# An attention and channel-mix kernel whose first six tiles are laid out by hand

## The chip, the cores and the metric

The kernel runs on one core of a Trainium2 chip. A core has five engines that work side by side: TensorE (PE; its weight loads are listed apart as PEld), VectorE (DVE), ScalarE (ACT), GpSimd (POOL) and SyncE (SP, which here only issues transfers). The metric is the device time of one execution, in microseconds (us), as the median of several runs.

## The reference

Attention over 4 sequences of 768 tokens with 8 heads of 64, then a channel mix of the kind that RWKV models use. Cut to what matters:

```python
# attention: q, k, v are (4, 8, 768, 64); n_global = 8, n_local = 96
scores = (1 / sqrt(64)) * q @ k.transpose()
keep = is_global | is_local                # the first 8 keys, and the 96 keys up to the query
scores = where(keep, scores - slopes[h] * dist, -1e9)
a = exp(scores - max(scores))
a = a / (sum(a) + 1e-9)
x = a @ v                                  # heads side by side: (4, 768, 512)

# channel mix: w_k (512, 1024), w_r (512, 512), w_v (1024, 512), all float64
x_prev = x shifted by one token (0 before the first)
xk = mu_k * x + (1 - mu_k) * x_prev
xr = mu_r * x + (1 - mu_r) * x_prev
out = sigmoid(xr @ w_r) * (relu(xk @ w_k)**2 @ w_v)
```

## The kernel before

**Attention** goes by 24 tiles of 128 queries, each in four pairs of heads (hp). Tile n has 128 new keys; its window is 256 keys wide (128 where a sequence begins): the 32 first of the sequence, 96 before the tile, and its own. In the first 7 tiles ("native") queries and keys are float32 on 64 of 128 partitions (`qz`, `kz`; the other 64 rows are zero), and each tile loads its own 128 keys and those before anew into its half of a two-buffer `kz`. For a pair, `scores` makes the product (L287), DVE adds the bias and finds the maximum (L295, `e<-s,pat`), ACT takes exp and its sum (L296). After every second pair DVE forms r = 1 / (sum + 1e-9) (L302, L303) and POOL multiplies the four e by it (L306). `transposes` turns e on PE (`t`, L317) and ACT copies it out of PSUM (`et`, L318); `weighted` multiplies with v (`av`, L334), and ACT copies a tile's `av` to `x` (L345).

**The weights** come as float64 and are taken apart by bit operations in 20 steps of 128x512: 8 of w_k, 4 of w_r, 8 of w_v. `weight_begin` loads the raw words, ACT takes |top| times a power of two (L166, L169), then POOL (L167, first 8) or DVE (L170, the other 12) scales or bounds it, and DVE makes three bit operations: a shift (L171), the sign (L172) and the low word's bits (L173). ACT or POOL rounds the result to float32r, the hi part; `weight_end` has POOL subtract for the lo part (L180). `weights_go` sets how many are begun and ended after each slot.

**The channel mix** goes by 12 chunks of 256 tokens. `mix` makes xk and xr from x (POOL L357, or ACT for chunk 0; DVE L358), with hi (L359) and lo parts (L360). Each product is three matmuls, hi with hi, hi with lo and lo with hi (L371 to L373): 96 for xk @ w_k (`kp`), then relu and square (L397, L398), 24 for xr @ w_r (`z`), 48 for the product with w_v (`vps`), and the output (L414). This is a generator that yields 40 times in a chunk.

**What sets the order.** The main loop has 25 steps of four slots; slot = 4 * step + hp. In each slot come, in the program, the transposes of the tile before, the scores of this tile and then up to 5 yields of channel mix, by a budget (`run_ffn(2.5)` twice). Chunk c's mix is queued at hp 0 of step 2c + 3; for the first, the budget begins at -17.5. From this program a scheduler with a timeline of its own sets the order of each engine's instructions: one may go ahead of those written before it. Waits between engines follow from the buffers: among others 3 PSUM tiles of the pool `f` (kp, z, vps), 2 for the transposes and 1 for av; and the 3 buffers of `p4k` in SBUF, which the mixes, the queries and keys from tile 7 on and the raw w_r and w_v weights share.

Of the kernel before, what the change touches and what calls it, by code (L numbers as in the profile page):

```python
# [33 lines left out]
def tile_biased_attention_channel_mix(ctx: ExitStack, tc: tile.TileContext, qT, kT, v, n_sizes, mu_kr, w_k, w_v, w_r, q_rows, k_rows, v_rows, slopes, out):  # L34
    nc = tc.nc
    vec, act, pool, pe = nc.vector, nc.scalar, nc.gpsimd, nc.tensor
# [106 lines left out]

    def weight_begin(i):
        # A float64 weight's words: (sign, 11 exponent bits, 20 bits), (32 bits).
        # a: its first 24 significant bits as a float32; hi: a rounded to float32r; lo: the rest of a.
# [1 line left out]
        if name != "k":
            raw = p4k.tile([128, 512, 2], I32, tag="t4k", name=f"w64_{i}")
            a = f2_pool.tile([128, 512], I32, tag="f2", name=f"wa_{i}")  # L150
        elif k < 2:
            both = f_pool.tile([128, 2048], I32, tag=("kk_hi", "kk_lo")[k], name=f"w64_{i}")
            raw = both[:, 0:1024].rearrange("p (n w) -> p n w", w=2)
            a = both[:, 1024:1536]
        else:
            t = "xk" if k == 2 else "xr"
            raw = f_pool.tile([128, 512, 2], I32, tag=t + "_hi", name=f"w64_{i}")
            a = f_pool.tile([128, 512], I32, tag=t + "_lo", name=f"wa_{i}")
        nc.sync.dma_start(raw.rearrange("p n w -> p (n w)"), src[k * 128 : (k + 1) * 128, 2 * c : 2 * c + 1024])
# [4 lines left out]
        # or the min) to a large number, under 2**-127 (by underflow or the max) to 0.
        if i < 8:
            act.activation(a.bitcast(F32), top.bitcast(F32), AF.Abs, scale=2.0**111)  # L166
            pool.tensor_scalar(a.bitcast(F32), a.bitcast(F32), 2.0**-112, 2.0**-111, op0=ALU.mult, op1=ALU.mult)  # L167
        else:
            act.activation(a.bitcast(F32), top.bitcast(F32), AF.Abs, scale=2.0**16)  # L169
            vec.tensor_scalar(a.bitcast(F32), a.bitcast(F32), 2.0, HUGE, op0=ALU.max, op1=ALU.min)  # L170
        vec.tensor_scalar(a, a, 3, 0x7FFFFFF8, op0=ALU.logical_shift_left, op1=ALU.bitwise_and)  # L171
        vec.scalar_tensor_tensor(a, top, -0x80000000, a, op0=ALU.bitwise_and, op1=ALU.bitwise_or)  # L172
        vec.scalar_tensor_tensor(a, low, 29, a, op0=ALU.logical_shift_right, op1=ALU.bitwise_or)  # L173
# [8 lines left out]
    w_count = [0, 0]  # L182

    def weights_go(begun, ended):
        while w_count[0] < min(begun, len(w_steps)):
            weight_begin(w_count[0])
            w_count[0] += 1
        while w_count[1] < min(ended, w_count[0]):
            weight_end(w_count[1])
            w_count[1] += 1  # L190
# [8 lines left out]
    state = {}  # L199
    # the first tiles' queries and keys, with 64 rows of zeros: products of all 128 rows keep the tensor engine's clock up  # L200
    padded = []
    for i in range(2):
        qz = q_pool.tile([128, H, 128], F32, name=f"qz_{i}", tag="qh")
        kz = kw_pool.tile([128, H, 256], F32, name=f"kz_{i}", tag="kw")
        pool.memset(qz[64:128], 0.0)
        pool.memset(kz[64:128], 0.0)
        padded.append((qz, kz))
# [431 lines left out]
```

## Time and profile before

| what | value |
|---|---|
| median of 3 runs | 526.14 us (525.98 to 527.11) |
| span of the profiled execution | 524.1 us, 9900 instructions |
| PE busy | 495.9 us (95%) |
| DVE busy | 372.4 us (71%) |
| ACT busy | 323.6 us (62%) |
| POOL busy | 283.0 us (54%) |
| data moved | 48.16 MB, 92 GB/s over the span |

The profiled execution is one run of its own, and all places in time below are from its start. An engine's busy share is a mean over the whole span; where in the span an engine is full, and where another waits for it, is read from slices and windows. PE's instructions overlap, so the time of one in a row is read from its start to the start of the next. A row names the line of the program, the engine, the operation, then output and inputs by the program's names with their shapes.

### The profile page before, as it was taken

Reading aid. Unit: us, or ns where it says so; the run is one execution under the profiler, and the core shown is the slowest. Engines: PE = TensorE matmul, PEld = TensorE weight load, DVE = VectorE, ACT = ScalarE, POOL = GpSimd, SP = SyncE. Lnnn points to the kernel's source line nnn. Section 1 sums busy time; section 2 is a strip of 40 time slices with the busy share of each in tenths; the row PEclk is TensorE's granted clock in tenths of the full one; section 3 lists DMA queues with packets and bytes.
Section 4 is the critical chain, followed back from the end, with each engine's and each line's share of the span. In section 5 each row is a group of like instructions: output and inputs, shape, how many; then the busy total and the mean of one; then the engine's idle time right before and its main releaser. Section 6 shows DMA issues by size and latency. Waiting matters only on the chain.

```text
span 524.1 us, 9900 instructions
## 1 busy us (share of the span) xinstructions
PE 495.9 (95%) x3466; PEld 427.2 (82%) x3466; DVE 372.4 (71%) x854; ACT 323.6 (62%) x730; POOL 283.0 (54%) x410
## 2 busy tenths in 40 slices
PE   7885888979999999999999999999999999999995
PEld 4563766869898898898898898898898898898984
DVE  6799999987677766767767867767777865535321
ACT  4868585823957856846847757756757667643220
POOL 8799977987355644544547645535547634203000
PEclk9979799999999999999999999999999999999999
DMA  8998268150350530530521431521422210000101
GB/s 197 322 232 198 67 185 188 41 144 20 107 134 6 141 107 5 157 91 8 162 76 38 130 86 34 133 86 59 124 62 66 62 46 26 35 12 2 41 1 44
DMA packets 27304, 48.16 MB, mean 92 GB/s; under 512 B 7216, under 2 KB 13360, under 8 KB 27248
## 3 DMA queue, kind: packets, MB, share of 16 engines
q1 hardware_dynamic: 27104, 47.46, 34.0%
q8 instruction: 29, 0.48, 0.4%
q14 instruction: 27, 0.22, 0.1%
q10 hardware_dynamic: 144, 0.00, 0.0%
HBM read 41.16 MB, written 6.29 MB: 91 GB/s over the span
## 4 chain that ended last, share of the span: by engine, by line
PE 80%; DVE 11%; POOL 5%; issue 3%; DMA 1%; ACT 0%; DVEq 0%; POOLq 0%
PE vps L372 8%; PE vps L373 8%; PE vps L371 8%; PE kp L371 8%; PE kp L373 8%; PE kp L372 8%; PE av L334 7%; PE t L317 6%; PE z L371 4%; PE z L373 4%; PE z L372 4%; PE s L290 3%; PE s L289 3%; POOL e L306 2%; PE s L287 2%
## 5 line engine op out<-in xcount | busy, mean ns | idle before, releaser
L306 POOL TENSOR_SCALAR e<-e,r 128x256 f32<-128x256 f32 (+1 forms) x192 | 106.1, 570 | 137.0 <-DVE r L303 91.9
L371 PE MATMUL kp<-xk_hi,wk_hi 128*128 128x256 f32 x384 | 108.0, 282 | 0.2 <-DVE kk L398 0.2
L373 PE MATMUL kp<-xk_hi,wk_lo 128*128 128x256 f32 x384 | 107.5, 280 | 0.5 <-POOL wk_lo L180 0.5
L372 PE MATMUL kp<-xk_lo,wk_hi 128*128 128x256 f32 x384 | 107.3, 279 | 0.0
L296 ACT ACTIVATE e<-e,nmax 128x256 f32<-128x256 f32 (+1 forms) x192 | 92.6, 484 | 22.0 <-DVE nmax L295 21.0
L295 DVE CUSTOM_DVE_ANT_0 e<-s,pat 128x256 f32<-128x256 f32 (+1 forms) x192 | 69.0, 395 | 31.0 <-PE s L290 21.2
L372 PE MATMUL vps<-wv_lo,kk_hi 128*128 128x512 f32 x192 | 76.0, 396 | 2.6 <-POOL wv_lo L180 2.6
L371 PE MATMUL vps<-wv_hi,kk_hi 128*128 128x512 f32 x192 | 75.9, 395 | 0.4 <-POOL wv_hi L196 0.4
L373 PE MATMUL vps<-wv_hi,kk_lo 128*128 128x512 f32 x192 | 75.8, 395 | 0.0
L371 PEld LDWEIGHTS kp<-xk_hi,wk_hi 128*128 128x128 f32 x384 | 72.9, 190 | 1.2 <-DVE kk L398 0.6
L373 PEld LDWEIGHTS kp<-xk_hi,wk_lo 128*128 128x128 f32 x384 | 72.8, 190 | 0.9 <-POOL wk_lo L180 0.9
L372 PEld LDWEIGHTS kp<-xk_lo,wk_hi 128*128 128x128 f32 x384 | 72.9, 190 | 0.6
L318 ACT COPY et<-t 128x512 f32<-128x512 f32 (+1 forms) x96 | 52.0, 546 | 20.2 <-PE t L317 19.7
L317 PE MATMUL t<-ident,e 128*128 128x128 f32 x352 | 57.5, 280 | 5.7 <-POOL e L306 5.6
L398 DVE TENSOR_TENSOR kk<-kp,kk 128x512 f32<-128x512 f32 x48 | 33.1, 689 | 41.2 <-ACT kk L397 41.0
L317 PEld LDWEIGHTS t<-ident,e 128*128 128x128 f32 x352 | 41.2, 141 | 19.1 <-POOL e L306 9.2
L334 PE MATMUL av<-et,va 128*64 128x128 f32 x704 | 49.4, 284 | 0.6 <-ACT et L318 0.6
L334 PEld LDWEIGHTS av<-et,va 128*64 128x64 f32 x704 | 40.3, 139 | 10.5 <-issue 5.8
L400 DVE TENSOR_TENSOR kk_lo<-kk,kk_hi 128x512 fp32r<-128x512 f32 x48 | 35.3, 735 | 17.4 <-ACT kk_hi L399 17.3
L399 ACT CAST kk_hi<-kk 128x512 fp32r<-128x512 f32 x48 | 29.8, 622 | 25.6 <-DVE kk L398 25.6
L397 ACT ACTIVATE kk<-kp 128x512 f32<-128x512 f32 x48 | 28.3, 590 | 26.7 <-PE kp L373 24.5
L372 PEld LDWEIGHTS vps<-wv_lo,kk_hi 128*128 128x128 f32 x192 | 36.0, 187 | 10.5 <-POOL wv_lo L180 3.1
(103 smaller groups left out, 1051.1 us busy)
## 6 DMA issues: line engine op xcount, KB each, us to landing
kraw<-in_kT_dram SPq DMA_DIRECT2D x36, 256.0 KB, 3.9
qraw<-in_qT_dram SPq DMA_DIRECT2D x34, 256.0 KB, 4.1
va<-in_v_dram SPq DMA_DIRECT2D x24, 256.0 KB, 3.1
out_dram<-sig SPq DMA_DIRECT2D x24, 256.0 KB, 3.5
w<-in_w_k_dram SPq DMA_DIRECT2D x8, 512.0 KB, 9.1
w<-in_w_v_dram SPq DMA_DIRECT2D x8, 512.0 KB, 3.5
kz<-in_kT_dram SPq DMA_DIRECT2D x8, 256.0 KB, 6.7
w<-in_w_r_dram SPq DMA_DIRECT2D x4, 512.0 KB, 9.3
```

What stands on the lines that cost most here:

```text
L295: vec.tensor_tensor_reduce(out=e[:, :w], in0=o, in1=p[:, h, :], op0=ALU.add, op1=ALU.min, scale=-0.125, scalar=3.0e38, accum_out=s["nmax"] ...
L296: act.activation(e[:, :w], e[:, :w], AF.Exp, bias=s["nmax"][:, h : h + 1], scale=-1.0, accum_out=s["sum"][:, h : h + 1])
L306: pool.tensor_scalar(e[:, :w], e[:, :w], r[:, u : u + 1], 1.0, op0=ALU.mult, op1=ALU.mult)
L317: pe.transpose(pt[:, c : c + 128], e[:, k * 128 : (k + 1) * 128], ident)
L318: act.copy(et[:, : 2 * nb * 128], pt[:, : 2 * nb * 128])
L334: pe.matmul(o, vt[:, h * 64 : (h + 1) * 64], et[:, c : c + 128], start=k == 0, stop=k == nb - 1)
L371: pe.matmul(o, sh, mh, start=first, stop=False)
L372: pe.matmul(o, sh, ml, start=False, stop=False)
L373: pe.matmul(o, sl, mh, start=False, stop=last)
L398: vec.tensor_mul(kk, pv, kk)
L399: act.copy(kkh[:, 2 * fp : 2 * fp + 2, :], kk)
L400: vec.tensor_sub(kkl[:, 2 * fp : 2 * fp + 2, :], kk, kkh[:, 2 * fp : 2 * fp + 2, :])
```

## The change

It has seven parts.

1. DVE, ACT, POOL and SP are reached through a class `InOrder`; while its flag is on (slots 0 to 23, tiles 0 to 5) each of their instructions stays in the order in which the program is written. PE is still ordered by the scheduler. Since all calls pass through the class, their rows bear its one line, L46.
2. The weights go in four stages (load, begin, bits, end), each paced by a table, `w_pace`: a weight a slot up to slot 8, more behind it. Raw words are loaded three weights ahead.
3. The bits of a weight go through a PSUM tile, `wb`, of the pool `f`: the shift writes it, the sign operation reads and writes it, the last reads it and writes SBUF. All 20 weights are begun on ACT and POOL; L170 is gone.
4. In tiles 0 to 7 e is not multiplied by r. Instead r (128 queries x 8 heads) is spread by eight small products with the identity (`rb`), ACT copies that to SBUF (`rs`), and DVE multiplies `av` by it on the way to x, in place of ACT's copy.
5. The keys of tiles 0 to 6 lie in a ring of three tiles and are loaded once. POOL copies the 32 first keys aside (`k_glob`) and over the first 32 of the tile before. A head's scores are two products of 128 columns.
6. Chunk 0's mix is made in two halves of 128 tokens, through PSUM (`mix_first`), at slots 8 and 11. Up to step 8 a tile's av is made in its own next step, pair by pair; chunk c's channel mix is queued at slot 4 * (2c + 2) + 3 (c up to 3) or, later, at hp 0 of step 2c + 3; the budget starts at 0 for chunk 0 and at -10 for chunk 1.
7. A tile's queries and keys are loaded two steps ahead.

```diff
+EARLY = 8
+class InOrder:
+    on = True
+    def __getattr__(self, name):
+        f = getattr(self.engine, name)
+        def call(*args, **kwargs):
+            ins = f(*args, **kwargs)
+            if InOrder.on:
+                self.tc.keep_in_program_order(ins)
+            return ins
+        return call
...
+    def weight_load(i):
+        name, src, k, c = w_steps[i]
+        if i >= 7:
+            raw = p4k.tile([128, 512, 2], I32, tag="t4k", name=f"w64_{i}")
...
+    def weight_bits(i):
...
-        if i < 8:
-            act.activation(a.bitcast(F32), top.bitcast(F32), AF.Abs, scale=2.0**111)
-            pool.tensor_scalar(a.bitcast(F32), a.bitcast(F32), 2.0**-112, 2.0**-111, op0=ALU.mult, op1=ALU.mult)
-        else:
-            act.activation(a.bitcast(F32), top.bitcast(F32), AF.Abs, scale=2.0**16)
-            vec.tensor_scalar(a.bitcast(F32), a.bitcast(F32), 2.0, HUGE, op0=ALU.max, op1=ALU.min)
-        vec.tensor_scalar(a, a, 3, 0x7FFFFFF8, op0=ALU.logical_shift_left, op1=ALU.bitwise_and)
-        vec.scalar_tensor_tensor(a, top, -0x80000000, a, op0=ALU.bitwise_and, op1=ALU.bitwise_or)
-        vec.scalar_tensor_tensor(a, low, 29, a, op0=ALU.logical_shift_right, op1=ALU.bitwise_or)
+        bits = ps_f.tile([128, 512], I32, name=f"wb_{i}", tag="f")
+        vec.tensor_scalar(bits, a, 3, 0x7FFFFFF8, op0=ALU.logical_shift_left, op1=ALU.bitwise_and)
+        vec.scalar_tensor_tensor(bits, top, -0x80000000, bits, op0=ALU.bitwise_and, op1=ALU.bitwise_or)
+        vec.scalar_tensor_tensor(a, low, 29, bits, op0=ALU.logical_shift_right, op1=ALU.bitwise_or)
...
+    k_ring = [kz[0][:, 0], kz[0][:, 1], kz[1][:, 0]]
+    k_glob = kz[1][:, 1, :, 0:GMAX]
...
+            if t == 0:
+                pool_copy(k_glob[0:64], s["kr"][0:64, :, 0:GMAX])
+            elif t > 1:
+                pool_copy(state[n - 1]["kr"][0:64, :, 0:GMAX], k_glob[0:64])
...
-                pe.matmul(o, s["qr"][:, h, :], s["kr"][:, h, c0:256], start=True, stop=True)
+                for i, m in enumerate((n - 1, n) if t else (n,)):
+                    pe.matmul(o[:, i * 128 : (i + 1) * 128], s["qr"][:, h, :], state[m]["kr"][:, h, :], start=True, stop=True)
...
+        if n < EARLY:
+            if hp == 3:
+                r = s["r"] = s_pool.tile([128, H], F32, name=f"r_{n}", tag="rr")
+                vec.tensor_scalar(r, s["sum"], 1.0e-9, None, op0=ALU.add)
+                vec.reciprocal(r, r)
+            return
...
+        if hp == 2 and n < EARLY:
+            rb = ps_t.tile([128, 4, 128], F32, name=f"rb_{n}", tag="t")
+            for h in range(H):
+                a, o = divmod(h, 2)
+                pe.matmul(rb[64 * o : 64 * o + 64, a, :], s["r"][:, h : h + 1].to_broadcast([128, 64]), ident, start=True, stop=True)
+            s["rs"] = et_pool.tile([128, 4, 128], F32, name=f"rs_{n}", tag="et")
+            act.copy(s["rs"], rb)
...
+            if n < EARLY:
+                vec.tensor_mul(xo, av, s["rs"])
+            else:
+                act.copy(xo, av)
...
+    def mix_first(i):
...
+        for tag in "kr":
+            tmp[tag] = ps_f.tile([128, 4, 128], F32, name=f"mixp_{tag}", tag="f")
+            for j in range(4):
+                act.activation(tmp[tag][:, j, :], x[:, j, 128 * i : 128 * i + 128], AF.Copy, scale=mu[tag][1][:, j : j + 1])
+        for tag in "kr":
+            for j in range(4):
+                vec.scalar_tensor_tensor(tmp[tag][:, j, :], x[:, j, 128 * i + 1 : 128 * i + 129], mu[tag][0][:, j : j + 1], tmp[tag][:, j, :], op0=ALU.mult, op1=ALU.add)
+        for tag in "kr":
+            act.copy(first_mix[tag][0][:, :, c], tmp[tag])
+        for tag in "kr":
+            vec.tensor_sub(first_mix[tag][1][:, :, c], tmp[tag], first_mix[tag][0][:, :, c])
...
+    def go_ffn(c):
+        queue.append(ffn(c))
+        if c == 1:
+            budget[0] = -10.0
+    def w_pace(slot):
+        return slot + 1 if slot < 8 else 8 + (slot - 7) * 4 // 3 if slot < 11 else 12 + (slot - 10) * 8 // 5
...
+            slot = 4 * step + hp
+            InOrder.on = slot < 24
+            if step <= EARLY:
+                weights_go(3, w_pace(slot - 2))
+                weights_go(1, w_pace(slot))
+                if step:
+                    transposes(step - 1, hp)
+                weights_go(2, w_pace(slot - 1))
+                scores(step, hp)
+                if slot == 8:
+                    mix_first(0)
+                if step:
+                    for i in ([] if hp == 0 else [hp - 1]) + ([3] if hp == 3 else []):
+                        weighted(step - 1, i)
+                    if hp == 3:
+                        global_v(step)
+                        if step % 2 == 0:
+                            go_ffn(step // 2 - 1)
...
+            if hp == 3 and step + 2 < NTILES:
+                load_tile(step + 2)
+            if hp == 3 and 2 < step + 1 < NTILES:
+                load_v(step + 1)
+            weights_go(0, w_pace(slot) + 3)
```

How the order moves, at three places.

On PE, at the first `kp` (numbers behind the names are the program's own). Before:

```order
L334 MATMUL av_729<-et_3_676,va_413 64x128
L317 MATMUL t_0_750<-ident,e_0_582 128x128 x2
L371 MATMUL kp<-xk_hi,wk_hi 128x256 x2
L317 MATMUL t_0_750<-ident,e_1_585 128x128 x2
L317 MATMUL t_1_812<-ident,e_2_634 128x128 x2
L317 MATMUL t_1_812<-ident,e_3_637 128x128 x2
L372 MATMUL kp<-xk_lo,wk_hi 128x256
L373 MATMUL kp<-xk_hi,wk_lo 128x256
```

And after the change:

```order
L381 MATMUL av_505<-et_3_557,va_201 64x128
L356 MATMUL t_0_683<-ident,e_0_444 128x128 x2
L356 MATMUL t_0_683<-ident,e_1_447 128x128 x2
L356 MATMUL t_1_751<-ident,e_2_499 128x128 x2
L356 MATMUL t_1_751<-ident,e_3_502 128x128 x2
L441 MATMUL kp<-xk_hi,wk_hi 128x256
L442 MATMUL kp<-xk_lo,wk_hi 128x256
L443 MATMUL kp<-xk_hi,wk_lo 128x256
```

Before, the av of tiles 0 to 2 and the scores of tiles 0 to 3 and of three quarters of tile 4 stand ahead of the first kp, and 48 kp follow before the next attention. Now tiles 0 and 1 whole, tile 2's scores and half of its transposes stand ahead of it, and 72 kp follow.

On DVE, between the last e ahead of the first kp's inputs and the first result of kp. Before (w_5, wa_355 and wa_505 are weights):

```order
L172 SCALAR_TENSOR_TENSOR wa_355<-w_7_354,wa_355 128x512
L302 TENSOR_SCALAR r_3_691<-sum_476 128x4
L170 TENSOR_SCALAR wa_505<-wa_505 128x512
L173 SCALAR_TENSOR_TENSOR wa_355<-w_7_354,wa_355 128x512
L303 RECIPROCAL r_3_691<-r_3_691 128x4
L360 TENSOR_TENSOR xk_lo<-mix_k,xk_hi 128x1024
L171 TENSOR_SCALAR wa_505<-wa_505 128x512
```

And after (wb is a weight's bits in PSUM, w_12 the raw words of the thirteenth weight):

```order
L46 RECIPROCAL r_584<-r_584 128x8
L46 TENSOR_TENSOR x_415<-av_505,rs_596 128x4x128
L46 SCALAR_TENSOR_TENSOR mixp_k<-x_415,mus,mixp_k 128x128 x4
L46 SCALAR_TENSOR_TENSOR mixp_r<-x_415,mus,mixp_r 128x128 x4
L46 TENSOR_TENSOR xk_lo<-mixp_k,xk_hi 128x4x128
L46 TENSOR_TENSOR xr_lo<-mixp_r,xr_hi 128x4x128
L46 TENSOR_TENSOR kk<-kp,kk 128x512
L46 TENSOR_TENSOR kk_lo<-kk,kk_hi 128x512
L46 TENSOR_SCALAR wb_690<-wa_553 128x512
```

Before, the bits of the weights 5, 7 and 11 lie around xk_lo and go on behind it; now the bits of all twelve w_k and w_r weights stand ahead of it, and w_v's behind the first kk.

On PE, at the last chunk's kp near the end, behind the av of the last tile. Before:

```order
L371 MATMUL vps<-wv_hi,kk_hi 128x512
L372 MATMUL vps<-wv_lo,kk_hi 128x512
L373 MATMUL vps<-wv_hi,kk_lo 128x512
L371 MATMUL kp<-xk_hi,wk_hi 128x256
L372 MATMUL kp<-xk_lo,wk_hi 128x256
```

And after:

```order
L441 MATMUL vps<-wv_hi,kk_hi 128x512
L442 MATMUL vps<-wv_lo,kk_hi 128x512
L443 MATMUL vps<-wv_hi,kk_lo 128x512
L441 MATMUL kp<-xk_hi,wk_hi 128x256 x3
L442 MATMUL kp<-xk_lo,wk_hi 128x256
```

Between the last av and this kp, 6 z and 48 vps stood before; now 15 vps do.

More of the change, by code (lines that the diff above doesn't have):

```diff
@@ L142, in tile_biased_attention_channel_mix @@
     w_live = {}
-    def weight_begin(i):
-        name, src, k, c = w_steps[i]
[L148 to L154, printed above, removed]
-        else:
[L156 to L159, printed above, removed]
+    w_raw = {}
@@ new lines, in weight_load @@
+    def weight_load(i):
+        name, src, k, c = w_steps[i]
+        if i >= 7:
+            raw = p4k.tile([128, 512, 2], I32, tag="t4k", name=f"w64_{i}")
+        elif i < 3:
+            raw = p4k.tile([128, 512, 2], I32, tag="t4k", name=f"w64_{i}")
+        else:
+            both = f_pool.tile([128, 1024 if i < 5 else 2048], I32, tag=("xk_hi", "xr_hi", "kk_lo", "kk_hi")[i - 3], name=f"w64_{i}")
+            raw = both[:, 0:1024].rearrange("p (n w) -> p n w", w=2)
+        sync.dma_start(raw.rearrange("p n w -> p (n w)"), src[k * 128 : (k + 1) * 128, 2 * c : 2 * c + 1024])
+        w_raw[i] = raw
@@ L180, in weight_end, with weights_go @@
         pool.tensor_sub(lo, w_live.pop(i).bitcast(F32), hi)
[L182 to L190, printed above, removed]
+    w_stages = (weight_load, weight_begin, weight_bits, weight_end)
+    w_count = [0, 0, 0, 0]
+    def weights_go(stage, n):
+        while w_count[stage] < min(n, len(w_steps)):
+            w_count[stage] += 1
+            w_stages[stage](w_count[stage] - 1)
     def weights_need(n):
-        weights_go(n, n)
+        for stage in range(4):
+            weights_go(stage, n)
     def pool_copy(dst, src):
@@ L199, in tile_biased_attention_channel_mix @@
     state = {}
-    padded = []
+    qz = [q_pool.tile([128, H, 128], F32, name=f"qz_{i}", tag="qh") for i in range(2)]
+    kz = [kw_pool.tile([128, 2, H, 128], F32, name=f"kz_{i}", tag="kw") for i in range(2)]
     for i in range(2):
[L203 to L207, printed above, removed]
+        pool.memset(qz[i][64:128], 0.0)
+        pool.memset(kz[i][64:128], 0.0)
@@ L463, in tile_biased_attention_channel_mix @@
                 split_tile(step + 1)
[L464 to L466 removed]
+            if hp == 3 and step + 2 < NTILES:
[3 more added lines that the diff above has]
+            weights_go(0, w_pace(slot) + 3)
     for i in range(4):
         weighted(NTILES - 1, i)
[L469 to L470 removed]
+    go_ffn(NCHUNK - 1)
     while queue:
```

127 lines of the change are left out of this document (69 added, 58 removed).

## The prediction

> **What bounds the kernel now.** I read the page's span and its forty slices first, then a table of windows cut where TensorE's state changes, then the groups of the first 117 us. The page:
>
> ```profile
> span 524.1 us, 9900 instructions
> ...
> PE   7885888979999999999999999999999999999995
> ```
>
> A slice is 13.1 us, a digit its busy tenths. PE is at 9 from the tenth slice to the last but one, and below it before. In windows (columns: start:end and length, then busy us and count of PE, PEld, DVE, ACT, POOL, granted clock, DMA share, GB/s):
>
> ```profile
> 0.00:54.80 54.80, 41.10 (x209) 27.69 (x209) 47.00 (x149) 38.42 (x111) 47.94 (x67) 0.91 0.96 227
> 54.80:65.00 10.20, 8.62 (x57) 7.95 (x56) 8.92 (x18) 5.19 (x15) 10.20 (x12) 0.83 0.26 86
> 65.00:78.00 13.00, 11.32 (x88) 8.76 (x87) 13.00 (x35) 10.48 (x26) 9.07 (x11) 1.00 0.62 169
> 78.00:91.00 13.00, 10.49 (x90) 8.85 (x89) 13.00 (x28) 7.07 (x21) 9.97 (x12) 1.00 0.83 200
> 104.00:117.00 13.00, 9.91 (x61) 7.87 (x61) 11.50 (x15) 1.80 (x3) 10.36 (x11) 1.00 0.46 122
> 117.00:518.50 401.50, 401.49 (x2912) 355.62 (x2908) 265.26 (x588) 249.12 (x534) 183.37 (x287) 1.00 0.25 69
> ```
>
> The first cut is the first channel-mix product (kp) at 54.8. In the start VectorE (DVE) and GpSimd (POOL) are busier than PE: it is theirs, the rest is PE's. Behind it PE idles 1.58 + 1.68 + 2.51 + 3.09 = 8.9 us in four of the windows up to 117 (it is full in the one left out, 91 to 104), and none from 117 to 518.5. So the span is T0, the start of the first kp, plus the PE work behind it, plus PE's waits behind it. Before: 54.8 + 469.3. What fills the start (busy us and mean ns of one, then the idle time before):
>
> ```profile
> L306 POOL TENSOR_SCALAR e<-e,r 128x256 f32<-128x256 f32 x40 | 32.0, 814 | 8.4 <-DVE r L303 8.4
> L173 DVE SCALAR_TENSOR_TENSOR wa<-w,wa 128x512 int32<-128x512 int32 x16 | 15.1, 948 | 0.0
> L172 DVE SCALAR_TENSOR_TENSOR wa<-w,wa 128x512 int32<-128x512 int32 x16 | 12.6, 795 | 0.1
> L171 DVE TENSOR_SCALAR wa<-wa 128x512 int32<-128x512 int32 x16 | 8.5, 535 | 0.0
> ```
>
> POOL's normalisation of e and DVE's bit operations are the two large blocks, and both are edited.
>
> **The change in terms of this sum.** It shortens the start (no L306 in eight tiles, no L170, bits through PSUM, one load per key), fixes DVE's, ACT's and POOL's order to the 24th slot, and starts chunk 0's channel mix a slot earlier in the program, behind two whole tiles of attention where before four tiles' scores stood. What leaves the path ahead of T0 in this way has to be done behind it, where PE is the bound.
>
> *Work behind T0.* PE's rows:
>
> ```profile
> 25.03 1.03 PE L287 MATMUL s<-kz,qz 128*128 128x256 f32 x4
> 25.99 0.66 PE L334 MATMUL av<-et,va 128*64 128x128 f32 x8
> 54.79 0.48 PE L371 MATMUL kp<-xk_hi,wk_hi 128*128 128x256 f32 x2
> 59.38 0.41 PE L373 MATMUL kp<-xk_hi,wk_lo 128*128 128x256 f32 x1
> 59.59 0.41 PE L371 MATMUL kp<-xk_hi,wk_hi 128*128 128x256 f32 x1
> 63.07 0.28 PE L373 MATMUL kp<-xk_hi,wk_lo 128*128 128x256 f32 x1
> 63.19 0.28 PE L371 MATMUL kp<-xk_hi,wk_hi 128*128 128x256 f32 x1
> 93.17 0.60 PE L287 MATMUL s<-kz,qz 128*128 128x128 f32 x4
> 93.61 0.60 PE L317 MATMUL t<-ident,e 128*128 128x128 f32 x4
> 94.14 0.65 PE L334 MATMUL av<-et,va 128*64 128x128 f32 x4
> 166.99 1.95 PE av L334 x32
> ```
>
> From start to start, a score instruction of 256 columns takes 0.24 us (0.96 / 4) and one of 128 columns 0.11; a tile has 16 or 32 of them, 3.84 or 3.52 us. A transpose takes 0.13 (0.53 / 4), an av instruction 0.061 (1.95 / 32). Behind T0 now come 1.75 more tiles of scores (tile 3 and three quarters of tile 4, 6.7 us), ten transposes (1.25) and tile 2's av (1.95): +9.9. The product of r with the identity has the shape of an av instruction: 16 in a tile, six tiles behind T0, 16 x 6 x 0.061 = +5.9. Splitting the scores saves 0.32 in each of tiles 3 to 5: -1.0. Off go the waits of before, 8.9, and its slow kp: 33 at 0.21 (59.38 to 59.59) where one takes 0.12 (63.07 to 63.19), 3.1 us. So 469.3 - 12.0 + 9.9 + 5.9 - 1.0 = 472.1, and the span after is **T0 + 472.1 + S**, S being PE's new waits and slow stretches. It is even with before at T0 + S = 52.0.
>
> *T0.* In DVE's new order the first kp stands behind the bits of all twelve w_k and w_r weights, though the first kp reads only w_k's. DVE's rows:
>
> ```profile
> 9.78 0.28 DVE L295 CUSTOM_DVE_ANT_0 e<-s,pat 128x128 f32<-128x128 f32 x1
> 9.99 0.28 DVE L295 CUSTOM_DVE_ANT_0 e<-s,pat 128x128 f32<-128x128 f32 x1
> 41.33 0.41 DVE L295 CUSTOM_DVE_ANT_0 e<-s,pat 128x256 f32<-128x256 f32 x1
> ...
> 41.68 0.41 DVE L295 CUSTOM_DVE_ANT_0 e<-s,pat 128x256 f32<-128x256 f32 x1
> 54.27 0.41 DVE L170 TENSOR_SCALAR wa<-wa 128x512 f32<-128x512 f32 x1
> 54.60 0.68 DVE L173 SCALAR_TENSOR_TENSOR wa<-w,wa 128x512 int32<-128x512 int32 x1
> 55.20 0.17 DVE L303 RECIPROCAL r<-r 128x4 f32<-128x4 f32 x1
> ```
>
> An e takes 0.21 or 0.35; with nothing beside it L170 takes 0.33 and L173 0.60. No row has the bits in PSUM. Below: the first of the three keeps the pace of a one-input operation in SBUF, 0.33 + 0.60 + 0.60 = 1.53 a weight. Above: nothing is gained on the means of the groups, 0.53 + 0.80 + 0.95 = 2.28. I take 0.61 for each, 1.83: L306 no longer runs beside them, and one that writes or reads PSUM is nearest to L173 alone.
>
> The Trainium skill ("VectorE: DVE Perf Modes", section "Why PSUM operands drop a tier") speaks against this part of the change: a float32 operation with an operand in PSUM loses the double rate that one wholly in SBUF can have. By it the first of the three costs 0.61 and not 0.33, some 3.4 us over twelve weights. The same skill ("SBUF — State Buffer", section "Who interferes with whom") has DVE and GpSimd shut each other out where DVE reads two SBUF inputs; the 948 of L173 beside POOL against 600 alone agrees, and PSUM takes one of the inputs away.
>
> DVE begins on e at 9.3 (two e of 0.21 before the second row, with their start-up). To the end of xk_lo it has 12 x 1.83 = 22.0 of bits, 8 x 0.21 + 16 x 0.35 = 7.3 of e, 0.6 of r, two x products at an e's pace per column (1.2), 16 mixes of 128 columns (3.4 at an e's 0.21), and three half-chunk differences at an L173's pace (1.9): 36.4. The first bits must wait for POOL, which has pat to do first:
>
> ```profile
> 9.82 1.72 POOL L137 TENSOR_SCALAR pat<-btmp 128x256 bf16<-128x256 f32 x4
> 14.02 0.62 POOL L167 TENSOR_SCALAR w<-w 128x512 f32<-128x512 f32 x1
> ```
>
> 11.5 + 0.6 = 12.1, while DVE has had only tile 0's first e: 2.2 us lost. Floor: 9.3 + 36.4 + 2.2 = 47.9. In a fixed order a late input stops everything behind it, on DVE the e of the next tile, and so ACT and PE too. I count the x product behind ACT's copy of the product with r (2 x 1.2), the half-chunk mixes that go ACT, DVE, ACT, DVE (2 x 1.3), and the twelfth weight's load, which waits for a buffer (1.0): 6. **T0 = 54**; bounds 49 (one wait of 1) and 58 (bits at 2.1).
>
> *S.* PE before the first kp has less to do than before, so I keep the slow clock behind it: 3.0 of the 3.1. Chunk 1's mix begins only when tile 3's av is copied, and two kp stand in PE's order ahead of tile 5's scores. The end of before shows how long such a mix takes:
>
> ```profile
> 477.62 0.59 ACT L345 COPY x<-av 128x512 f32<-128x512 f32 x1 [1.42 <-PE av L334]
> 478.38 2.17 POOL L357 TENSOR_SCALAR mix_k<-x,mus 128x256 f32<-128x256 f32 x4 [19.85 <-ACT x L345]
> 481.47 1.05 ACT L359 CAST xk_hi<-mix_k 128x1024 fp32r<-128x1024 f32 x1 [1.59 <-DVE mix_k L358]
> 483.22 1.21 DVE L360 TENSOR_TENSOR xk_lo<-mix_k,xk_hi 128x1024 fp32r<-128x1024 f32 x1
> ```
>
> From the last av (477.5) to xk_lo (484.4) pass 6.9 us; the two hi products can go first, and half of it is covered by transposes and scores: 3.6 for chunk 1, 1.0 for chunk 2, which has more between. At the end the work between the last av and kp was 12.6 us (6 z of 0.23, 48 vps, 16 av); now 15 vps are left, 3.5 us of cover for the same 6.9 less 0.4 of hi products: 2.9. The w_v weights are bitten off earlier than before (by slot 16), 0.5. S = 3.0 + 3.6 + 1.0 + 2.9 + 0.5 = **11**, bounds 6 (no slow clock, chunk 1 at half) and 14.
>
> The keys ring (POOL copies of 64x256, two or three a tile, at L306's per-column price under 0.4 us each) and the loads two steps ahead I cost at nothing: POOL is rid of 32 us of L306, and a tile's loads end long before its scores. If POOL's cover were gone they would cost about 2 us.
>
> Span 54 + 472.1 + 11 = 537.1. The profiled execution lies 2.0 under the median of the runs (524.1 against 526.1), so **539.1 us**.
>
> **Rivals.**
>
> *The start really shrinks: faster.* The bits run at 1.53 (3.6 us less than I took), the fixed order has hardly any wait, since the freed POOL has each weight ready before DVE's turn for it: T0 = 45. PE then comes to kp without a pause, so no slow clock, and only the end's 3: S = 3. 45 + 472.1 + 3 = 520.1, so 522. For it: DVE is 47.0 of 54.8 busy in the first window and even at 1.83 a weight's bits cost it 0.45 less than on the means, besides L170. Against it: twelve weights stand where only part had to be done.
>
> *The gain is paid back exactly: no change.* T0 at the floor 47.9 and S = 4: 524.0, so 526.
>
> *The raw loads set the pace: slower by more.* From the eighth weight on all raw words pass through the four-kilobyte buffers that the queries, keys and mixes use too:
>
> ```profile
> w<-in_w_r_dram SPq DMA_DIRECT2D x4, 512.0 KB, 9.3
> ```
>
> With about 9 us from issue to landing and three in flight, one weight comes every 3.1 us where four must come between slots 8 and 11; in DVE's fixed order e waits behind them. Twelve weights at 3.1 from the start of the fifth (about 24 us): T0 = 24 + 8 x 3.1 + 12 for the rest = 61, S = 12: 545, so 547, and up to 553 if w_v's follow suit. For it: the first window's DMA share is 0.96. Against it: w_k's load ahead by three slots, and each tile now loads 256 columns of queries and keys where it loaded 384.
>
> That the change doesn't do what it says needs no own rival: its order is fixed in the program.
>
> **Chances.** The forecast's case 0.53 (its own range 531 to 546: T0 + S from 57 to 72), the faster one 0.25, no change 0.06, slower by more 0.16. What a measurement of this kernel can tell is about 0.2%, 1.05 us. Faster 0.25, within 0.06, slower 0.69. For eight in ten the range reaches into the faster case down to 520 and to 552 above, leaving a tenth on each side.
>
> **What would show it.** The first kp's start says T0: under 48 and the faster rival is on. The mean of the three bit operations says 1.53, 1.83 or 2.28. PE's idle time between T0 and 150 us, and the granted clock there, say S; so does the wait of the first kp after the last av (0 before, 2.9 by me). A DVE wait put down to a DMA of w in the first 50 us speaks for the loads. I am wrong in the main if PE has no waits behind T0, or if DVE reaches xk_lo before 46.

## The result and the profile after

The changed kernel takes 578.4 us (577.29 to 580.68, 5 runs) against 526.14 us (525.87 to 527.11, 5 runs): a ratio of 1.099, 95% interval 1.097 to 1.102. It is slower, as forecast, but by 52 us where 13 were said, and outside the range. The page of its profiled execution, the span and the engines' busy tenths:

```profile
span 578.8 us, 10185 instructions
...
PE   5775686979999999999999999999999999999896
PEld 2654575768878889889879889888888898898784
DVE  5959467455538839667578487577586774650530
ACT  3656444545475665756745955766657558552230
POOL 8643224431015354454374456264544743420300
```

A slice is now 14.5 us. Through the first nine slices no engine is full for long: DVE, at 9 in six slices on end before, is at 3 to 5 in eight of its first twelve, and POOL at 5 or below from the third to the sixteenth. So DVE and POOL no longer fill the start, and PE doesn't either. The windows say where PE loses (columns as in the prediction; the first cut is the first kp):

```profile
0.00:64.40 64.40, 38.91 (x203) 29.01 (x203) 47.69 (x136) 36.70 (x101) 37.61 (x54) 0.68 0.59 180
64.40:77.00 12.60, 11.71 (x80) 11.18 (x80) 5.39 (x10) 4.04 (x7) 2.12 (x4) 0.76 0.04 11
77.00:100.00 23.00, 15.52 (x115) 13.58 (x112) 15.47 (x32) 10.53 (x25) 8.19 (x10) 0.88 0.27 91
100.00:126.00 26.00, 26.00 (x171) 21.26 (x169) 12.25 (x35) 14.06 (x34) 7.43 (x9) 0.91 0.22 62
126.00:140.00 14.00, 9.15 (x62) 8.35 (x61) 9.15 (x21) 5.73 (x13) 6.70 (x12) 0.76 0.31 81
140.00:525.00 385.00, 383.62 (x2801) 334.46 (x2800) 252.27 (x592) 246.00 (x545) 174.01 (x268) 1.00 0.29 76
525.00:545.00 20.00, 17.18 (x103) 13.97 (x102) 7.94 (x12) 4.36 (x6) 4.49 (x8) 0.91 0.08 27
545.00:573.20 28.20, 28.07 (x155) 24.43 (x154) 6.40 (x11) 6.08 (x10) 0.00 (x0) 0.94 0.03 11
```

T0 is 64.4, and 514.4 us follow it, so S is 514.4 - 472.1 = 42.3. PE idles 17.5 us behind T0 (0.89 + 7.48 + 4.85 + 1.38 + 2.82 + 0.13, the length less the busy time of each window, up to 573.2), and a granted clock under 1.00 in six windows is worth up to 15 us more (length times what is missing: 3.0 + 2.8 + 2.3 + 3.4 + 1.8 + 1.7), about 12 of it by busy time in place of length. Between 77 and 100 us PE and DVE are each busy for 15.5 of 23.0 us: neither is full.

What they wait for, first DVE from 66 to 140 us, then ACT and PE from 64 to 140 (us in total, times, longest):

```profile
DVE kk L46 <- ACT kk L46: 10.9, 5, 5.0
DVE e L46 <- PE s L320: 7.5, 3, 4.3
DVE r L46 <- ACT e L46: 5.7, 2, 3.7
```

```profile
ACT kk L46 <- PE kp L443: 5.6, 2, 5.1
ACT wa L46 <- DMA w<-in_w_v_dram: 5.4, 2, 5.2
```

```profile
PE kp L441 <- ACT xk_hi L46: 8.2, 2, 4.1
PE z L441 <- DVE wa L46: 4.7, 1, 4.7
PE av L381 <- ACT et L46: 2.3, 1, 2.3
```

Of PE's two waits for xk_hi (8.2) one, of 4.0, ends at 64.4 with the first kp itself and belongs to T0; only the second, of 4.1 at chunk 1's first kp, lies behind it. DVE stands at kk while PE makes 72 kp in a row, then at e while PE has not made its scores; ACT stands for 5.2 us at a w_v weight whose words are not there; and z waits 4.7 us for the last bit operation (wa) of a weight: both z and a weight's bits take a tile of the pool f.

### The profile page after: what moved, and what is told of

The parts are those of the page before. It is cut to its first block, busy times and chain, and to the rows that moved or that the text cites. A ratio compares the mean times of both kernels' runs of the same rounds, so it can differ in the third digit from the quotient of the medians.

```text
span 578.8 us, 10185 instructions
## 1 busy us (share of the span) xinstructions
PE 530.2 (92%) x3674; PEld 456.2 (79%) x3674; DVE 357.2 (62%) x844; ACT 327.5 (57%) x740; POOL 240.6 (42%) x364
## 5 line engine op out<-in xcount | busy, mean ns | idle before, releaser
L441 PE MATMUL kp<-xk_hi,wk_hi 128*128 128x256 f32 x384 | 111.2, 295 | 10.4 <-ACT xk_hi L46 9.4
L46 ACT ACTIVATE e<-e,nmax 128x256 f32<-128x256 f32 (+1 forms) x192 | 92.7, 484 | 38.0 <-DVE nmax L46 37.0
L442 PE MATMUL kp<-xk_lo,wk_hi 128*128 128x256 f32 x384 | 110.7, 290 | 3.3 <-DVE xk_lo L46 3.3
L46 POOL TENSOR_SCALAR e<-e,r 128x256 f32<-128x256 f32 (+1 forms) x128 | 61.7, 501 | 124.6 <-DVE r L46 112.5
L443 PE MATMUL kp<-xk_hi,wk_lo 128*128 128x256 f32 x384 | 109.5, 287 | 0.0
L46 DVE CUSTOM_DVE_ANT_0 e<-s,pat 128x256 f32<-128x256 f32 (+1 forms) x192 | 68.2, 394 | 60.3 <-PE s L323 36.7
L441 PEld LDWEIGHTS kp<-xk_hi,wk_hi 128*128 128x128 f32 x384 | 74.4, 196 | 14.8 <-ACT xk_hi L46 11.0
L442 PEld LDWEIGHTS kp<-xk_lo,wk_hi 128*128 128x128 f32 x384 | 75.3, 196 | 5.3 <-DVE xk_lo L46 4.3
L443 PEld LDWEIGHTS kp<-xk_hi,wk_lo 128*128 128x128 f32 x384 | 75.1, 196 | 0.2 <-issue 0.2
L381 PE MATMUL av<-et,va 128*64 128x128 f32 x704 | 55.1, 289 | 8.4 <-ACT et L46 8.4
L46 ACT COPY et<-t 128x512 f32<-128x512 f32 (+1 forms) x96 | 51.5, 544 | 17.9 <-PE t L356 17.7
L46 DVE TENSOR_TENSOR kk<-kp,kk 128x512 f32<-128x512 f32 x48 | 33.1, 690 | 37.1 <-ACT kk L46 36.7
L46 ACT CAST kk_hi<-kk 128x512 fp32r<-128x512 f32 x48 | 29.8, 621 | 42.4 <-DVE kk L46 42.4
L356 PEld LDWEIGHTS t<-ident,e 128*128 128x128 f32 x352 | 42.4, 144 | 13.4 <-issue 5.3
L46 DVE TENSOR_TENSOR kk_lo<-kk,kk_hi 128x512 fp32r<-128x512 f32 x48 | 34.5, 718 | 22.1 <-ACT kk_hi L46 22.1
L320 PE MATMUL s<-kz,qz 128*128 128x128 f32 x192 | 35.2, 346 | 11.9 <-DVE nmax L46 7.7
```

Source lines behind the costliest of these rows:

```text
L46: ins = f(*args, **kwargs)
L320: pe.matmul(o[:, i * 128 : (i + 1) * 128], s["qr"][:, h, :], state[m]["kr"][:, h, :], start=True, stop=True)
L356: pe.transpose(pt[:, c : c + 128], e[:, k * 128 : (k + 1) * 128], ident)
L381: pe.matmul(o, vt[:, h * 64 : (h + 1) * 64], et[:, c : c + 128], start=k == 0, stop=k == nb - 1)
L441: pe.matmul(o, sh, mh, start=first, stop=False)
L442: pe.matmul(o, sh, ml, start=False, stop=False)
```

## The experiments

Times are medians, ratios are against the kernel before on the same chip; spans are of profiled executions. Differences within the changed kernel are against its span of 578.8 unless it is said otherwise. That execution was the slowest of five (their median span is 576.5), so where the medians of the times give another difference, it stands beside.

**1. No fixed order.**

```diff
-    InOrder.on = True
     load_tile(0)
...
-            InOrder.on = slot < 24
```

> The changed kernel with the flag of the class off everywhere, so that the scheduler orders DVE, ACT, POOL and SP again; all else stays. Theory 'fixed order' (late inputs stop DVE and ACT, so PE waits and slows): PE's waits behind the first kp fall from 17.4 us to about 9, as before the change, and the span from 578.8 to about 545. Rival 'content' (the new operations and the earlier channel mix cost it, whoever orders them): the span stays above 565.

547.35 us, span 547.2. The fixed order is worth 31.6 of the 54.7 us (by the times 31.1 of 52.3). The first kp comes later (75.2), and chunk 0's last vps no earlier (120.6 against 119.9), but chunk 1's first kp starts 17.5 us sooner; with the fixed order and then without:

```profile
130.33 0.80 PE L441 MATMUL kp<-xk_hi,wk_hi 128*128 128x256 f32 x2 [4.13 <-ACT xk_hi L46]
```

```profile
112.86 0.39 PE L441 MATMUL kp<-xk_hi,wk_hi 128*128 128x256 f32 x1
```

At chunk 3's first kp it is 31.8 us (221.4 against 189.6), which is the whole difference. A late first kp is no loss if PE has other work ahead of it: 531 of its instructions stand there in this run, 203 with the fixed order.

**2. The bits in SBUF.**

```diff
-        bits = ps_f.tile([128, 512], I32, name=f"wb_{i}", tag="f")
+        bits = a
```

> The changed kernel with the three bit operations in SBUF again. Theory 'PSUM is the dearer place': a weight's bits fall from 2.09 us to about 1.6 and z's wait of 4.7 us for a PSUM tile goes; first kp at about 59, span about 568. Rival 'PSUM keeps DVE clear of POOL': the bits rise to about 2.3, the first kp stays at 64 or comes later, span 576 to 584.

586.72 us, span 585.3, the first kp at 70.8. The rival holds, with a span 1.3 above what it named. The groups of the first 117 us with PSUM, and then with SBUF:

```profile
L46 DVE SCALAR_TENSOR_TENSOR wb<-w,wb 128x512 int32<-128x512 int32 x20 | 13.9, 696 | 0.7
L46 DVE TENSOR_SCALAR wb<-wa 128x512 int32<-128x512 int32 x20 | 13.7, 687 | 2.2 <-POOL wa L46 2.2
L46 DVE SCALAR_TENSOR_TENSOR wa<-w,wb 128x512 int32<-128x512 int32 x20 | 13.7, 687 | 0.7
...
L46 POOL TENSOR_SCALAR wa<-wa 128x512 f32<-128x512 f32 x20 | 12.3, 621 | 38.4 <-ACT wa L46 38.1
```

```profile
L46 DVE SCALAR_TENSOR_TENSOR wa<-w,wa 128x512 int32<-128x512 int32 x39 | 38.7, 991 | 1.3
L46 POOL TENSOR_SCALAR wa<-wa 128x512 f32<-128x512 f32 x20 | 16.8, 842 | 36.9 <-ACT wa L46 36.3
L46 DVE TENSOR_SCALAR wa<-wa 128x512 int32<-128x512 int32 x20 | 9.4, 472 | 2.2 <-POOL wa L46 2.2
```

In SBUF the operation with one input is quicker (472 against 687 ns), but those with two SBUF inputs slow to 991 from 690, and POOL's operation from 621 to 842. Both pages cited in the prediction say so: the Trainium skill's "VectorE: DVE Perf Modes" (section "Why PSUM operands drop a tier") for the first, its "SBUF — State Buffer" (section "Who interferes with whom") for the second, and here the second weighs more. z's wait for wa went, as the theory said, and 6.5 us were lost all the same.

**3. e multiplied by r on POOL, in the fixed order.** So in all three places:

```diff
-            if n < EARLY:
+            if n < 0:
```

> The changed kernel with e multiplied by r on POOL in tiles 0 to 7 as before, without the product of r with the identity (PE loses 8 us of work) and with ACT's copy to x. Theory 'fixed order': POOL's 64 operations stand in its fixed order ahead of the weights' steps, so the first kp comes some 5 us later and the span stays at 575 to 585. Rival 'content': span about 570, by the 8 us of PE.

590.3 us, span 589.6, first kp at 70.4. The first kp comes 6 us later, as the theory said, but the span is above what either account named. In the fixed order the product of r is worth 11 us although, by the prediction's 0.061 an instruction, it costs PE 8.

**4. PE kept busy in the start.**

```diff
+        if 4 * n + hp < 10:
+            for u in range(2):
+                for _ in range(2):
+                    pe.matmul(pt[:, 0 : 128 * nb], ident, s["e"][2 * hp + u][:, 0 : 128 * nb], start=True, stop=True)
```

> The changed kernel with added products on PE: in the first ten slots of transposes, each e is multiplied four times in all by the identity into the same PSUM tile ahead of its transposes (the results are overwritten). Theory 'clock' (PE idles so much in the start that its clock halves, and its halved work is what the others wait for): granted clock near 1.0 before the first kp, which comes at 58 or sooner, and span 565 or less. Rival 'DVE sets the start': the clock rises, but the first kp stays within 2 us of 64.4, and the span falls by at most 6 us (the slow products just behind it).

579.76 us, span 577.3. Its first window:

```profile
0.00:64.80 64.80, 46.80 (x282) 36.91 (x282) 47.89 (x136) 36.83 (x101) 37.53 (x54) 0.92 0.59 180
```

The granted clock rises from 0.68 to 0.92, and the first kp stays at 64.8. The rival holds: the slow clock of the start is a mark of waiting, not its cause.

**5. The fixed order up to the first kp alone.**

```diff
-            InOrder.on = slot < 24
+            InOrder.on = slot < 12
```

> The changed kernel with the fixed order for slots 0 to 11 alone (up to the first channel-mix product) instead of 0 to 23. Theory 'the order costs where PE already has channel mix to do': the first kp stays at about 64, and the span falls by most of the 31 us that the order costs, to 555 or less. Rival 'the order costs in the start, by the late first kp and what hangs on it': the span stays above 570.

553.47 us, span 551.6. The first half of the fixed order costs 4.4 us against none (551.6 against 547.2), the second half 27.2; by the times it is 6.1 and 24.9. The theory's span holds, but not its place of the first kp, which moves from 64.4 to 70.3 although the slots ahead of it are still fixed; the trace doesn't say why. From the first kp to 140 us:

```profile
70.30:140.00 69.70, 69.58 (x508) 60.49 (x507) 48.09 (x104) 47.02 (x95) 25.15 (x32) 1.00 0.33 91
```

PE is full at full clock where the changed kernel idles 13.2 us between 64.4 and 140 at a clock of 0.76 to 0.91.

**6. and 7. DVE's order alone, and all but DVE's.** The first of the two edits; the second wraps the other three engines in its place.

```diff
-    vec, act, pool, sync = (InOrder(tc, e) for e in (nc.vector, nc.scalar, nc.gpsimd, nc.sync))
+    vec = InOrder(tc, nc.vector)
+    act, pool, sync = nc.scalar, nc.gpsimd, nc.sync
```

> The changed kernel with the fixed order on DVE alone (slots 0 to 23); ACT, POOL and SP are the scheduler's. Theory 'DVE's fixed order is the cause, since e, kk and the weights' bits queue behind each other's inputs there': the span stays at 570 or more. Rival 'it takes all four, ACT above all, which waits in order for raw w_v loads': span 550 to 558.

> The changed kernel with the fixed order on ACT, POOL and SP, and DVE the scheduler's. Theory 'DVE's order is the cause': span 550 to 558. Rival 'ACT's order is': 570 or more.

563.71 us (span 562.7) and 568.26 us (566.9). Neither account holds, here or there: DVE's order costs 15.5 us by itself (against 547.2), that of the other three 19.7, both 31.6 (by the times 16.4, 20.9 and 31.1). So the loss isn't DVE's alone, and ACT, POOL and SP were not tried apart.

**8. No fixed order, and e on POOL.** The edits of 1. and 3. together.

> The changed kernel without any fixed order, and with e multiplied by r on POOL in tiles 0 to 7 as before. Theory 'where the scheduler is free, the product of r is PE work that nothing hides': 8 us less on PE, span about 539 to 542 against 547.2. Rival 'POOL is the bound of the start': POOL's 32 us come back into the start, span 550 or more.

544.47 us, span 542.2. Taking the product of r out gains 5.0 us by the spans and 2.9 by the times, less than the 8 that it was to cost PE: the theory has the sign and not the size, and the rival, at 550 or more, falls. What is left of the change still costs 18 us.

**9. The same with the bits in SBUF.** The edits of 1., 2. and 3. together.

> The changed kernel without a fixed order, with e multiplied by r on POOL as before and with the bits in SBUF: of the change, the paces of the weights and of the channel mix, the ring of keys and chunk 0's mix in halves are left. Theory 'PSUM bits cost the free order as much as they cost the kernel before (10 us)': span 530 to 534 against 542.2. Rival 'PSUM bits help, as in the fixed order': 545 or more.

547.75 us, span 547.2. Here too PSUM helps, by 3 us in the times and 5 in the spans. The theory had taken its 10 us from run 10, and falls.

**10. The kernel before with the bits through PSUM, and nothing else.**

```diff
-        vec.tensor_scalar(a, a, 3, 0x7FFFFFF8, op0=ALU.logical_shift_left, op1=ALU.bitwise_and)
-        vec.scalar_tensor_tensor(a, top, -0x80000000, a, op0=ALU.bitwise_and, op1=ALU.bitwise_or)
-        vec.scalar_tensor_tensor(a, low, 29, a, op0=ALU.logical_shift_right, op1=ALU.bitwise_or)
+        bits = ps_f.tile([128, 512], I32, name=f"wb_{i}", tag="f")
+        vec.tensor_scalar(bits, a, 3, 0x7FFFFFF8, op0=ALU.logical_shift_left, op1=ALU.bitwise_and)
+        vec.scalar_tensor_tensor(bits, top, -0x80000000, bits, op0=ALU.bitwise_and, op1=ALU.bitwise_or)
+        vec.scalar_tensor_tensor(a, low, 29, bits, op0=ALU.logical_shift_right, op1=ALU.bitwise_or)
```

> The kernel before with one edit: the three bit operations go through a PSUM tile of the pool f. Theory 'PSUM keeps DVE clear of POOL': the three cost about 2.1 us where they cost 2.28 and more beside POOL, the start shortens by 3 to 6 us, span 519 to 522. Rival 'the PSUM tiles are taken from kp and z': span 524 to 530.

536.12 us, span 534.4: 10 us slower, ratio 1.0195 (1.0165 to 1.0224), above what either account named. The operations do get shorter (677 to 687 ns), but the scheduler, free, puts the first kp at 93.0, and PE waits for e on POOL. PE's waits for POOL's e from 0 to 100 us, in the kernel before and then in this run:

```profile
PE t L317 <- POOL e L306: 5.6, 10, 1.2
```

```profile
PE t L318 <- POOL e L307: 12.5, 5, 4.4
```

By the times the same edit gains 3 to 8 us in the changed kernel's orders and loses 10 in this one. That the three PSUM tiles which bits share with kp, z and vps make the scheduler move kp is likely but not shown.

**11. The kernel before with the product of r in tiles 0 to 7, and nothing else.** The three pieces of the change's diff that ask for `n < EARLY`, put into it.

> The kernel before with one edit: in tiles 0 to 7 e is not multiplied by r on POOL; r goes through the product with the identity to DVE's product on the way to x. Theory 'POOL's 38 us in the start are worth more than PE's 8': the first kp comes 6 us sooner and the span is 518 to 523. Rival 'PE is the bound and 8 us are added': span 528 to 533.

528.34 us, span 525.2, ratio 1.0046 (1.0028 to 1.0063). Neither account: the first kp came 2 us later (56.9), PE idled 16.4 us in the first 117 where it idled 22.6 before, but in the steady part a kp took 117.8 ns from start to start, where it takes 114.7 before.

**12. The same with a wider r tile.**

```diff
-                r = s["r"] = s_pool.tile([128, H], F32, name=f"r_{n}", tag="rr")
+                r = s["r"] = s_pool.tile([128, 32], F32, name=f"r_{n}", tag="rr")[:, 0:H]
```

> The kernel before with the product of r in tiles 0 to 7, as in the run with that edit alone, but the r tile of 32 columns in place of 8, which moves the channel mix's tiles by 288 bytes; each engine's order is the same. There a kp took 117.8 ns from start to start, where it takes 114.7 in the kernel before. Theory 'the place of xk in SBUF sets the step of kp': 114.7 again, 3.4 us less, span about 521.8, faster than before. Rival 'what stands ahead of kp on PE sets it': 117.8 and span 525.2 stay.

**522.17 us, ratio 0.9913 (0.9896 to 0.9929): a little faster than both kernels.** 24 kp from a narrow run, then 24 from a wide one:

```profile
188.65 0.28 PE L390 MATMUL kp<-xk_lo,wk_hi 128*128 128x256 f32 x1
...
191.46 0.28 PE L390 MATMUL kp<-xk_lo,wk_hi 128*128 128x256 f32 x1
```

```profile
189.58 0.28 PE L390 MATMUL kp<-xk_lo,wk_hi 128*128 128x256 f32 x1
...
192.30 0.28 PE L390 MATMUL kp<-xk_lo,wk_hi 128*128 128x256 f32 x1
```

2.81 / 24 = 117 ns against 2.72 / 24 = 113 ns, with each engine's order the same and only the tiles behind r's pool 288 bytes further on. Between these two runs it is place that sets the step. Over 1152 kp that is 3.9 us of the 6.2 gained; the rest is not assigned.

**13. The changed kernel with the wider r tile.**

> The changed kernel with the r tile of 32 columns in place of 8, which moves the channel mix's tiles by 288 bytes; each engine's order is the same. Theory 'the place sets the step of kp here too': kp's step falls from 117.6 to about 114 ns and the span from 578.8 to about 575. Rival 'the place acts only together with what stands ahead of kp': 117.6 and 578 stay.

571.71 us, span 569.7, step 114.2 ns. The theory holds, and more: some 7 us by the times (571.71 against 578.4) and 9 by the spans, 3.9 of them by 1152 steps of kp at 3.4 ns less. The first kp also comes 1.7 us sooner, at 62.7, which this run doesn't explain.

**14. to 16. The weave of before, the ring of keys, and both**, in the kernel of 8. (no fixed order, e on POOL). For the weave a tile's av stands at the head of the step after next, chunk c is queued at step 2c + 3, and the budget starts at -17.5. For the ring each tile's keys are loaded into halves of its own:

```diff
-            s["qr"], s["kr"] = qz[n % 2], k_ring[n % 3]
-            dma(s["kr"][0:64], kT[n])
+            s["qr"], s["kr"] = qz[n % 2], kz[n % 2]
+            dma(s["kr"][0:64, 1], kT[n])
+            if t == 1:
+                dma(s["kr"][0:64, 0], kT[n - 1])
+            elif t:
+                dma(s["kr"][0:64, 0, :, 0:32], kT[n - t, :, :, 0:32])
+                dma(s["kr"][0:64, 0, :, 32:128], kT[n - 1, :, :, 32:128])
```

> The changed kernel without a fixed order, with e multiplied by r on POOL, and with the weave of the kernel before (a tile's av at the head of the step after next, chunk c's mix from step 2c + 3, the budget from -17.5). Left of the change: PSUM bits and the weights' paces, the ring of keys, chunk 0's mix in halves. Theory 'the earlier channel mix costs most of the 18 us that the free order without the product of r still has (542.2 against 524.1)': span 526 to 531. Rival 'the weights' way costs it': span 538 or more.

> The changed kernel without a fixed order, with e multiplied by r on POOL, and with each tile's keys loaded into a buffer of its own halves as before (scores still in two products). Theory 'the ring is near nothing': span 540 to 544. Rival 'POOL's copies over the tile before hold up the scores, which were waited for on POOL in the changed kernel': span 536 or less.

> As the run with the weave of the kernel before, and also without the ring of keys. If weave and ring cost apart from each other, the two differences from 542.2 add up here; by the theory of the weave the span is 525 to 530, by its rival 536 or more.

536.4 us (span 535.2), 543.99 (544.0) and 531.88 (528.2; its runs lie from 529.93 to 536.44). The earlier channel mix and av cost 8 us of the 18 by the times (544.47 to 536.4), so run 14 falls between its two accounts. Of these 3.3 are by kp's step, which is 114.7 again though the pools are as in 8.: what stands ahead of kp seems to set the step too, unless it changes which of a pool's buffers a tile gets. The ring by itself is nothing; together with the old weave its removal gives 4.5, with an uncertainty nearly as large. With both gone 5.5 us are left, for the weights' paces, their bits, chunk 0's mix in halves, scores in two products and loads two steps ahead, which no run takes apart.

**17. and 18. The kernel of 12. with the product of r in five or three tiles.** `EARLY` is 5, then 3.

> The kernel before with the product of r in tiles 0 to 4 alone and the r tile of 32 columns. Against eight tiles it takes some 1.0 us of PE off in each of the tiles 5 to 7, where PE is the bound. Theory 'r's product pays only while POOL is the bound': span 518 to 519, time 519 to 520.5. Rival 'POOL's e of the tiles 5 to 7 hold up the start again': 522 or more.

> The same with tiles 0 to 2 alone. By the theory 2.0 us less again if POOL keeps up (517 to 518.5); by the rival, POOL's e of tiles 3 and 4 stand in the start, and the time is 521 or more.

522.99 us, ratio 0.995 (0.992 to 0.998), and 525.47 us, ratio 0.999 (0.998 to 1.000). The rival's times hold: what PE should save doesn't show. Five tiles can't be told from eight (520.85 to 526.76 against 520.98 to 523.28), three are slower. PE's waits for POOL's e up to 140 us are 1.7 us with five tiles and 2.0 with three, where eight have none; that this is the whole reason is not shown.

## Why the prediction was wrong

**The direction** rested on T0 + S against 52.0, and on the count of work behind the first kp. Both stood: T0 + S is 106.7, and T0 alone is past 52.0. Behind the first kp the trace has ten transposes and 32 av more than before, 96 instructions of the product of r, and 96 scores of 128 columns in place of 20 of 256, as counted.

**T0** was given as 54 and is 64.4 (xk_lo, to which the sum went, ends at 65.8). The rows of DVE:

```profile
14.77 0.69 DVE L46 TENSOR_SCALAR wb<-wa 128x512 int32<-128x512 int32 x1
15.49 0.70 DVE L46 SCALAR_TENSOR_TENSOR wb<-w,wb 128x512 int32<-128x512 int32 x1
16.22 0.69 DVE L46 SCALAR_TENSOR_TENSOR wa<-w,wb 128x512 int32<-128x512 int32 x1
16.83 0.28 DVE L46 CUSTOM_DVE_ANT_0 e<-s,pat 128x128 f32<-128x128 f32 x1
...
58.83 0.90 DVE L46 TENSOR_SCALAR r<-sum 128x8 f32<-128x8 f32 x1 [0.82 <-ACT e L46]
59.76 0.20 DVE L46 RECIPROCAL r<-r 128x8 f32<-128x8 f32 x1
59.88 0.65 DVE L46 TENSOR_TENSOR x<-av,rs 128x512 f32<-128x512 f32 x1
62.18 1.53 DVE L46 SCALAR_TENSOR_TENSOR mixp_k<-x,mus,mixp_k 128x128 f32<-128x128 f32 x4 [1.65 <-ACT mixp_k L46]
...
65.12 0.68 DVE L46 TENSOR_TENSOR xk_lo<-mixp_k,xk_hi 128x512 fp32r<-128x512 f32 x1
```

Four terms were short. A weight's bits take 0.72 + 0.73 + 0.61 = 2.06 and not 1.83: an operation that reads what the one ahead of it wrote starts 0.72 after it, one that doesn't 0.61 (+2.8 over twelve). A mix of 128 columns takes 0.38 (1.53 / 4) and not an e's 0.21, by whose row I priced it (+2.7). r keeps DVE for 2.95 us in its three times (1.05 here, 58.83 to 59.88), not 0.2 each (+2.3). And the waits, foreseen as 2.2 + 6, are these from 9 to 70 us:

```profile
DVE mixp_k L46 <- ACT mixp_k L46: 3.9, 2, 2.3
DVE e L46 <- PE s L320: 3.2, 1, 3.2
DVE r L46 <- ACT e L46: 2.4, 3, 0.9
DVE wb L46 <- POOL wa L46: 2.2, 1, 2.2
```

11.7 in all (+3.5). POOL's first weight came as said; the half-chunk mixes took 3.9 for 2.6; the x product's 2.4 and the twelfth load's 1.0 were no waits of their own; r's and e's were not in the sum. e's 3.2 are scores that came late on PE, in part behind POOL's copy of keys in the ring:

```profile
38.18 5.27 PE L320 MATMUL s<-kz,qz 128*128 128x128 f32 x24 [1.65 <-POOL kz L46]
```

The copy itself takes 0.40. But it stands in POOL's fixed order behind a weight's hi part, which waits for DVE's last bit operation of that weight, while DVE's next e waits for the scores behind the copy:

```profile
37.15 0.62 POOL L46 TENSOR_SCALAR wk_hi<-wa 128x512 fp32r<-128x512 f32 x1 [1.76 <-DVE wa L46]
37.73 0.40 POOL L46 TENSOR_SCALAR kz<-kz 64x256 f32<-64x256 f32 x1
```

So the mechanism was right and its sizes were not: 36.4 us of work were 44.8 (65.8 - 9.3 - 11.7).

**S** was given as 11 with bounds 6 and 14, and is 42.3. This is the step that failed. Of its terms chunk 1's mix (3.6) measured 4.1, and the end (2.9) measured 1.29 + 1.53 = 2.8; these were right. For chunk 2's mix (1.0) no wait shows. The w_v weights (0.5) measured 4.7 in z's wait alone. The slow clock (3.0) measured 12 to 15, since it falls anew behind these waits; the end shows it, where it was not in the sum at all:

```profile
542.47 0.58 PE L442 MATMUL kp<-xk_lo,wk_hi 128*128 128x256 f32 x1 [1.53 <-DVE xk_lo L46]
542.85 0.41 PE L443 MATMUL kp<-xk_hi,wk_lo 128*128 128x256 f32 x1
543.06 0.41 PE L441 MATMUL kp<-xk_hi,wk_hi 128*128 128x256 f32 x1
```

0.21 a kp again, after 2.8 us of waiting. What I had left out altogether is that the fixed order goes on to slot 23, over the stretch in which PE has channel mix to do. I priced late inputs for DVE up to the first kp only, and took PE to be the bound behind it. Run 5 shows that this second half of the order holds 25 to 27 of the 41.7 us by which the span was missed. Then kp's step, 2.9 ns longer over 1152 kp, adds 3.3 us, which nothing in the profile of before foretold. Idle time, slow clock and step make 33 to 36 of the 42. Another term was put at nothing: an av was priced at 0.061 by a row of 32 in a block, and part 6 cuts them up. In the traces, behind the first kp, av stand in 55 blocks where they stood in 26. At full clock an av comes 0.056 after another, but what follows a block comes 0.20 after its last av, and what stands ahead of a block takes 0.09 longer (a kp 0.21). An estimate from these: 29 x 0.24 = 7 us, about what was left; no run tries this part alone.

**The bits in PSUM** were bounded by 1.53 and 2.28, and measured 2.06 within that. **The work behind T0**, 472.1, is borne out by the counts above, but not the price of av in short blocks, which S takes up here. **The ring at nothing**: its copies held scores up, for 1.65 us in the row above and 0.7 behind chunk 1's first kp; run 15 shows no gain without it where no order is fixed. The price of under 0.4 was right, but L306's row, 814 ns for 256 columns, doesn't give it. **The rival of the raw loads** was named at 547: ACT's 5.2 us for a w_v load shows its mechanism, but for w_r's weights, on which its price stood, ACT waited 1.2 us in the first 117. **The faster rival** needed T0 at 45 and no waits behind, and **no change** T0 at 47.9; neither came.

Both of my signs of the main case were right (a first kp over 48, waits behind T0), so the direction was no luck, though the sum under it held a quarter of the loss. The range should have been open above: its upper end came from the rival of the raw loads, and nothing in it priced the fixed order behind the first kp.

## What to carry to other kernels

Where one engine is the bound, an order fixed by hand on the others has to be priced over all of its length, not only up to the point that it is laid out for: while the bound engine's own order comes from elsewhere, each side's head of the queue can wait for the other, and then no engine is full. Where a scheduler works, try one part of a large change at a time: the product of r, with a wider r tile, was worth 0.9%, inside a change that lost 10%. And before a small edit is judged, look whether its tiles moved the others.

## What the runs showed of the hardware

In stretches of 20 kp and more without a break the mean step lies at 113.3 to 114.4 ns or at 117.2 to 120 ns. A shift of 288 bytes of the tiles moved most stretches from the second group to the first, about 4 us in all, in two kernels (runs 12 and 13) with no change in order. It is no simple rule of place: by the kernels' pools the channel mix's tiles lie 384 bytes, three times 128, further on in run 13 than in run 8, as they do in run 12 than in the kernel before. The second pair has nearly the same step (113 ns in the rows of 12., 114.7 on the mean before), the first hasn't (114.2 and 117.6), and run 14, with run 8's pools, has 114.7. The rule is open.

On DVE, a 128x512 operation that reads what the one just ahead wrote starts 0.03 us after its end (14.77 + 0.69 to 15.49), and one that doesn't 0.08 ahead of its end (16.22 + 0.69 to 16.83). In run 2, with the bits in SBUF, it is the same, so it is not PSUM that does it.

Near the end the granted clock is 1.00 up to 541.0 us, 0.64 from there to 542.5 and 0.50 up to 548.0, by windows of the changed kernel's trace, after waits of 1.29 and 1.53 us with three kp between them.
